# The q scores of an agent-attention kernel, each 126-token tile computed as four 32-column tiles of the array

## The chip, the cores and the metric

The kernel runs on one core of a Trainium2 chip. The metric is the device time of one execution in microseconds (us). The time before is 2154.62 us, the median of three runs (2154.03 to 2154.73). A profile of one execution, with a span of 2150.6 us from the first to the last instruction, is what the readings below come from.

The engines are named as the profile names them: PE is TensorE's matmul, PEld its weight load, DVE is VectorE, ACT is ScalarE, POOL is GpSimd and SP is SyncE, which issues DMAs.

## The reference

Attention through 49 agents, then a two-layer network on 49920 tokens of width 128:

```python
B, N, C = (4, 12480, 128)
n_agents = 49
def sm(a, b):
    s = scale * (a @ b.transpose(0, 2, 1))
    s = s - s.max(-1, keepdims=True)
    e = np.exp(s)
    return e / (e.sum(-1, keepdims=True) + 1e-09)
a2k = sm(agents, k)
agent_v = a2k @ v
q2a = sm(q, agents)
out = (q2a @ agent_v)
...
h = x @ w_in          # 128 x 2048
g = h - np.tanh(h)
return (g @ w_out)    # 2048 x 128
```

The change concerns `q @ agents.T`, the scores of each token against its batch's 49 agents ("q scores").

## The kernel before

The tokens of each of the four batches are cut into 25 blocks of 500 (the last has 480), 100 blocks in all. The main loop runs over blocks and, within a block, over eight pairs of 128-wide slices of the 2048 hidden columns. In a step `m1` computes the hidden slice pair `h` in PSUM from the block's q softmax `pT` (lines 534 and 535: a high and a low part of the combined weights, so that two fast matmuls stand for one exact one). `act` computes `z` on ScalarE and `g` on VectorE (lines 544 to 549), `high` rounds `g` to `gh` on GpSimd (line 578), `low` takes the difference `gl` on VectorE (line 583), and `m2` adds the three products of `gh` and `gl` with the high and low parts of `w_out` to the block's sum (lines 596 to 598). Every other block computes one pair in plain fp32 instead (line 594), without `gh` and `gl`.

Beside this stream run jobs, Python generators that are advanced by one `yield` a step. For each pair of blocks a q job (`q_softmax`) makes the softmax of eight tiles of 126 tokens: the scores on TensorE (line 490), their maximum "qm" on VectorE (line 498), a copy on ScalarE, the subtraction on GpSimd, the exponential, the sums "qs" and the division on VectorE (lines 505 to 508), and the split into "pp" (lines 511 and 513). Later jobs transpose "pp" to `pT` (line 521). While a batch's blocks run, further jobs compute the next batch's agent side: its key scores (line 278), transposes (line 329) and value sums (line 339). Lines 249 and 369 are the first batch's, before the main loop starts.

In line 490 the stationary operand is a 126-token piece of `qt` (128 x 126) and the moving one is `ag` (128 x 49). Both are fp32, and each such matmul leaves two records in the profile. In line 278 the keys' scores are written to two halves of the PSUM partitions, each from a 64-column stationary operand:

```python
to = ps[HALF * r : HALF * (r + 1), c * 128 : (c + 1) * 128]
nc.tensor.matmul(to, self.agz[:, b, :], kt[:, n // 2 * r + c, :], start=True, stop=True)
```

The PSUM tile `misc` has two buffers, shared by the block sums, the q scores, the transposes and the agent side. `h` has three. The order on each engine in the main part is made by a scheduler from the order of the code and from its own estimates of durations, so a changed instruction can move others.

Of the kernel before, what the change touches and what calls it, by code (L numbers as in the profile page):

```python
# [24 lines left out]
A = 49  # L25
A2 = 2 * A
EARLY = 11
HALF = 64
FF = 2048
NCH = FF // 128  # L30
TT = 126
# [6 lines left out]
BT = GT // 2  # L38
# [58 lines left out]
class Build:  # L97
# [19 lines left out]
    def constants(self):  # L117
        nc = self.nc
        c = self.const
        self.agz = c.tile([128, B, HALF], F32, tag="ag", name="ag")  # L120
        self.ag = self.agz[:, :, :A]
# [6 lines left out]
        self.sel = c.tile([128, A], F32, tag="sel", name="sel")  # L128
        for r in (slice(0, HALF), slice(HALF, 128)):
            nc.vector.tensor_copy(self.sel[r], self.ident[r, r.start : r.start + A])  # L130
# [3 lines left out]
        nc.vector.memset(self.mx, 0.0)  # L134
        self.w_in = c.tile([128, FF], F32, tag="w_in", name="w_in")
        self.wo_h = c.tile([128, NCH, C], F32R, tag="wo_h", name="wo_h")
# [58 lines left out]
    def phase1(self, b):  # L195
# [36 lines left out]
        def scores(g):  # L232
# [42 lines left out]
            for c in range(n // 2):  # L275
                for r in range(2):
                    to = ps[HALF * r : HALF * (r + 1), c * 128 : (c + 1) * 128]
                    nc.tensor.matmul(to, self.agz[:, b, :], kt[:, n // 2 * r + c, :], start=True, stop=True)  # L278
# [4 lines left out]
        def max_in():  # L283
            yield
            yield
            if b:
                m = self.small.tile([128, 1], F32, tag="mk", name="mk")
                top = self.small.tile([128, 1], F32, tag="mt", name="mt")
                nc.vector.tensor_reduce(m, st["mxp"], axis=AX.X, op=ALU.max)
                nc.vector.tensor_copy(top[:HALF], m[HALF:])  # L290
                nc.vector.tensor_tensor(m[:HALF], m[:HALF], top[:HALF], ALU.max)
                nc.vector.tensor_copy(m[HALF:], m[:HALF])
                st["mb"] = self.small.tile([128, 1], F32, tag="mn", name="mn")
# [148 lines left out]
    def project(self, b, bound):  # L442
        nc = self.nc

        def part(c, lo, hi):
            yield
            yield
            if c == 0:
                self.aw[b] = tuple(
                    self.keep.tile([128, FF], F32R, tag=t, name=t, bufs=2) for t in ("awh", "awl")  # L450
                )
# [32 lines left out]
    def q_softmax(self, halves, qt, res, TT=TT):  # L484
        nc = self.nc
        ps = self.misc()
        for t in range(GT):
            b, at, w = halves[t // BT]
            at += min(t % BT * TT, w - TT)
            nc.tensor.matmul(ps[:TT, t * A : (t + 1) * A], qt[:, at : at + TT], self.ag[:, b, :], start=True, stop=True)  # L490
            if t % BT == BT - 1:
                yield
        pv = ps[:TT, : GT * A].rearrange("p (t a) -> p t a", a=A)
        m = self.small.tile([128, GT], F32, tag="qm", name="qm")
        e = self.small.tile([128, GT, A], F32, tag="qe", name="qe")
        ev = e[:TT]
        s = self.small.tile([128, GT], F32, tag="qs", name="qs")
        nc.vector.tensor_reduce(m[:TT], pv, axis=AX.X, op=ALU.max)
        nc.scalar.copy(ev, pv)  # L499
        yield  # L500
        nc.gpsimd.tensor_tensor(ev, ev, m[:TT, :, None].broadcast_to([TT, GT, A]), ALU.subtract)  # L501
        yield
        nc.scalar.activation(ev, ev, AF.Exp, scale=SCALE)
        yield
        nc.vector.tensor_reduce(s[:TT], ev, axis=AX.X, op=ALU.add)
        nc.vector.tensor_scalar(s[:TT], s[:TT], EPS, None, ALU.add)
        nc.vector.reciprocal(s[:TT], s[:TT])
        nc.vector.tensor_tensor(ev, ev, s[:TT, :, None].broadcast_to([TT, GT, A]), ALU.mult)
        yield
        pp = self.small.tile([128, GT, A2], F32R, tag="pp", name="pp")  # L510
        nc.scalar.copy(pp[:TT, :, :A], ev)  # L511
        yield
        nc.gpsimd.tensor_tensor(pp[:TT, :, A:], ev, pp[:TT, :, :A].bitcast(F32), ALU.subtract)  # L513
        res.append(pp)
# [119 lines left out]
    def fast(self):  # L634
# [21 lines left out]
        with ExitStack() as first:  # L656
# [6 lines left out]

            self.wf = self.keep.tile([128, FF], F32R, tag="awh", name="awh", bufs=2).bitcast(F32)
            loads = []
# [237 lines left out]
```

## Time and profile before

| what | value |
|---|---|
| median of three runs | 2154.62 us |
| span of the profiled execution | 2150.6 us |
| TensorE busy | 2126.8 us, 99% of the span |
| VectorE busy | 1998.3 us, 93% |
| ScalarE busy | 1828.1 us, 85% |
| GpSimd busy | 1313.8 us, 61% |
| matmul records | 10859 |
| line 490: matmuls | 800 records, 93.4 us busy, mean 269 ns |
| line 490: weight loads | 800 records, 95.9 us busy, mean 190 ns |
| line 490's share of the chain that ended last | 4% |
| mean granted TensorE clock | 0.998 |

The runs' own time lies some 4 us above the span of the profiled execution, which starts at the first instruction and ends with the last. In the profile's rows "x16" is the count of records merged into one row, "128\*126 128x49 f32" is the array's active rows and columns and the moving operand. Matmul bars overlap: a bar lasts longer than the distance to the next start, and its end is modelled. A stretch of matmuls is therefore measured from start to start.

### The profile page before, as it was taken

The page shows a single profiled execution, that of the slowest core. Times are in us where ns is not written, and L with a number is a line of the kernel's source. Part 1 is how long each engine was busy: PE and PEld are TensorE (multiplying, and loading weights), DVE is VectorE, ACT ScalarE, POOL GpSimd, SP SyncE. Part 2 cuts the span into 40 slices and gives each one's busy share as a digit, 9 for nine tenths or more (in the row PEclk, how much of TensorE's full clock was granted, in tenths as well). Part 3 has the DMA queues.
Part 4 walks back from the last instruction along what each step waited for, and adds up shares of the span by engine and source line. Part 5 has one row for each costly group of instructions (what it writes and reads, how often), then busy time and mean ns, then how long its engine had stood idle before and what let it go on. Part 6 is the DMA issues. An engine that isn't in the chain of part 4 may idle for free.

```text
span 2150.6 us, 30293 instructions
## 1 busy us (share of the span) xinstructions
PE 2126.8 (99%) x10859; PEld 1713.6 (80%) x10859; DVE 1998.3 (93%) x2031; ACT 1828.1 (85%) x2136; POOL 1313.8 (61%) x858
## 2 busy tenths in 40 slices
PE   8999999999999999999999999999999999999998
PEld 7587878877877887888787778878878888888886
DVE  7999998889999998889999999988999999999998
ACT  3888888888888888888898888888889889899896
POOL 0365566556665565556675557655566767777666
PEclk9999999999999999999999999999999999999999
DMA  9321112110111111111002110111000000000000
GB/s 350 96 67 60 52 34 73 51 49 29 39 49 59 60 50 49 59 61 49 20 20 68 59 42 28 51 59 41 28 31 20 29 30 20 29 29 20 29 10 21
DMA packets 65325, 108.69 MB, mean 51 GB/s; under 512 B 3984, under 2 KB 44176, under 8 KB 65168
## 3 DMA queue, kind: packets, MB, share of 16 engines
q1 hardware_dynamic: 65168, 106.68, 15.1%
q8 instruction: 89, 1.46, 0.3%
q14 instruction: 68, 0.56, 0.1%
HBM read 81.10 MB, written 25.56 MB: 50 GB/s over the span
## 4 chain that ended last, share of the span: by engine, by line
PE 95%; DVE 2%; POOL 1%; issue 1%; ACT 0%; DMA 0%; POOLq 0%; SPq 0%; DVEq 0%
PE h L534 17%; PE h L535 16%; PE misc L598 16%; PE misc L596 15%; PE misc L597 15%; PE misc L594 4%; PE misc L490 4%; PE misc L339 2%; PE misc L278 2%; PE misc L521 1%; PE h L249 1%; POOL gh L578 1%; DVE g L549 1%; PE misc L329 1%; DVE gl L583 1%
## 5 line engine op out<-in xcount | busy, mean ns | idle before, releaser
L578 POOL TENSOR_SCALAR gh<-g 128x1000 fp32r<-128x1000 f32 (+1 forms) x743 | 1172.7, 1579 | 702.9 <-DVE g L549 357.9
L583 DVE TENSOR_TENSOR gl<-g,gh 128x1000 fp32r<-128x1000 f32 (+1 forms) x743 | 952.8, 1284 | 99.9 <-PE misc L598 58.9
L549 DVE TENSOR_TENSOR g<-h,z 128x1000 f32<-128x1000 f32 (+1 forms) x800 | 946.1, 1187 | 24.6 <-ACT z L546 20.6
L544 ACT ACTIVATE y<-h 128x1000 f32<-128x1000 f32 (+1 forms) x800 | 799.0, 1002 | 191.6 <-PE h L535 187.6
L546 ACT ACTIVATE z<-y 128x1000 f32<-128x1000 f32 (+1 forms) x800 | 828.8, 1040 | 21.2 <-DVE g L549 4.2
L534 PE MATMUL h<-pT,awh 98*128 98x500 f32 (+1 forms) x1600 | 662.1, 414 | 0.1
L535 PE MATMUL h<-pT,awl 98*128 98x500 f32 (+1 forms) x1600 | 623.1, 389 | 0.0
L598 PE MATMUL misc<-gl,wo_h 128*128 128x500 f32 (+1 forms) x1486 | 589.5, 397 | 3.7 <-DVE gl L583 3.7
L596 PE MATMUL misc<-gh,wo_l 128*128 128x500 f32 (+1 forms) x1486 | 579.0, 390 | 2.8 <-POOL gh L578 2.8
L597 PE MATMUL misc<-gh,wo_h 128*128 128x500 f32 (+1 forms) x1486 | 578.1, 389 | 0.0
L534 PEld LDWEIGHTS h<-pT,awh 98*128 98x128 f32 x1600 | 301.2, 188 | 77.4 <-issue 14.0
L535 PEld LDWEIGHTS h<-pT,awl 98*128 98x128 f32 x1600 | 303.0, 189 | 67.7 <-issue 14.7
L598 PEld LDWEIGHTS misc<-gl,wo_h 128*128 128x128 f32 x1486 | 279.1, 188 | 70.0 <-DVE gl L583 10.5
L596 PEld LDWEIGHTS misc<-gh,wo_l 128*128 128x128 f32 x1486 | 280.8, 189 | 62.6 <-POOL gh L578 7.8
L597 PEld LDWEIGHTS misc<-gh,wo_h 128*128 128x128 f32 x1486 | 279.7, 188 | 54.5
L501 POOL TENSOR_TENSOR qe<-qe,qm 126x392 f32<-126x392 f32 x50 | 69.7, 1395 | 65.3 <-ACT qe L499 65.3
L513 POOL TENSOR_TENSOR pp<-qe,pp 126x392 fp32r<-126x392 f32 x50 | 67.8, 1357 | 58.4 <-ACT pp L511 56.6
L490 PEld LDWEIGHTS misc<-ag,qt 128*126 128x126 f32 x800 | 95.9, 190 | 3.9
L490 PE MATMUL misc<-ag,qt 128*126 128x49 f32 x800 | 93.4, 269 | 0.0
L594 PE MATMUL misc<-g,wo_f 128*128 128x500 f32 (+1 forms) x196 | 89.9, 581 | 0.0
L754 ACT ACTIVATE o<-misc 128x500 f32<-128x500 f32 (+1 forms) x100 | 58.2, 582 | 21.7 <-PE misc L598 11.7
L526 ACT CAST pT<-misc 98x500 fp32r<-98x500 f32 (+1 forms) x100 | 56.7, 568 | 7.4 <-PE misc L521 6.5
(111 smaller groups left out, 840.5 us busy)
## 6 DMA issues: line engine op xcount, KB each, us to landing
kt<-kT SPq DMA_DIRECT2D x48, 512.0 KB, 3.7
qt<-qT SPq DMA_DIRECT2D x46, 500.0 KB, 3.4
outT<-o SPq DMA_DIRECT2D x46, 500.0 KB, 2.6
v<-v SPq DMA_DIRECT2D x36, 512.0 KB, 4.1
vt<-v SPq DMA_DIRECT2D x12, 512.0 KB, 7.1
raw<-w_in SPq DMA_DIRECT2D x4, 512.0 KB, 9.0
v<-w_out SPq DMA_DIRECT2D x4, 512.0 KB, 8.9
qt<-qT SPq DMA_DIRECT2D x4, 490.0 KB, 3.4
```

What stands on the lines that cost most here:

```text
L490: nc.tensor.matmul(ps[:TT, t * A : (t + 1) * A], qt[:, at : at + TT], self.ag[:, b, :], start=True, stop=True)
L534: nc.tensor.matmul(h[:, c, :w], aw[0][:A2, sl], pT[:A2, :w], start=True, stop=False)
L535: nc.tensor.matmul(h[:, c, :w], aw[1][:A2, sl], pT[:A2, :w], start=False, stop=True)
L544: nc.scalar.activation(self.pair(y), h, AF.Tanh, scale=TSC)
L546: nc.scalar.activation(z, y, AF.Square)
L549: nc.vector.tensor_tensor(self.pair(g), h, self.pair(z), ALU.mult)
L578: self.nc.gpsimd.tensor_scalar(gh, g, 1.0, 0.0, ALU.mult, ALU.add)
L583: self.nc.vector.tensor_tensor(gl, g, gh.bitcast(F32), ALU.subtract)
L594: nc.tensor.matmul(acc[:, :w], wf[:, c * C : (c + 1) * C], gh[:, x], start=first, stop=last)
L596: nc.tensor.matmul(acc[:, :w], self.wo_l[:, f, :], gh[:, x], start=first, stop=False)
L597: nc.tensor.matmul(acc[:, :w], self.wo_h[:, f, :], gh[:, x], start=False, stop=False)
L598: nc.tensor.matmul(acc[:, :w], self.wo_h[:, f, :], gl[:, x], start=False, stop=last)
```

## The change

Each matmul of line 490 becomes four, of 32, 32, 32 and 30 tokens, which write to partitions 0, 32, 64 and 96 onward of the same PSUM columns. The output partitions select a group of 32 columns of the array, so the four are column tiles with a stationary operand of 32 (30) columns each. The moving operand is the same 128 x 49 for all. The `yield` that stood between the first four and the last four token tiles goes behind all eight, so the number of yields stays two.

```diff
+QUART = 32
...
         for t in range(GT):
             b, at, w = halves[t // BT]
             at += min(t % BT * TT, w - TT)
-            nc.tensor.matmul(ps[:TT, t * A : (t + 1) * A], qt[:, at : at + TT], self.ag[:, b, :], start=True, stop=True)
-            if t % BT == BT - 1:
-                yield
+            for r in range(0, TT, QUART):
+                m = min(QUART, TT - r)
+                to = ps[r : r + m, t * A : (t + 1) * A]
+                nc.tensor.matmul(to, qt[:, at + r : at + r + m], self.ag[:, b, :], start=True, stop=True)
+        yield
+        yield
```

The lines behind it move down by four: line 490 is line 494 in the changed kernel, 498 is 502, 534 is 538, 583 is 587, 596 to 598 are 600 to 602.

On TensorE, in the middle of the main loop, a job's scores stood as one row of eight matmuls between two steps' work:

```order
L598 MATMUL misc<-gl,wo_h 128x500
L596 MATMUL misc<-gh,wo_l 128x500
L597 MATMUL misc<-gh,wo_h 128x500
L490 MATMUL misc<-ag,qt 126x49 x8
L534 MATMUL h<-pT,awh 128x500
L535 MATMUL h<-pT,awl 128x500
```

In the changed kernel the same place holds eight times the first two of these score rows (32 matmuls), and the next work behind them is often the block sum's instead of a new `h`:

```order
L601 MATMUL misc<-gh,wo_h 128x500
L494 MATMUL misc<-ag,qt 32x49 x3
L494 MATMUL misc<-ag,qt 30x49
...
L602 MATMUL misc<-gl,wo_h 128x500
L600 MATMUL misc<-gh,wo_l 128x500
```

So the eight stay together, as they did, with four times as many instructions. In two of the 50 jobs they don't. There four matmuls of the block sum stand between the first and the last part of the changed kernel's scores on TensorE:

```order
L602 MATMUL misc<-gl,wo_h 128x500
L600 MATMUL misc<-gh,wo_l 128x500
L601 MATMUL misc<-gh,wo_h 128x500
L602 MATMUL misc<-gl,wo_h 128x500
L494 MATMUL misc<-ag,qt 32x49 x3
L494 MATMUL misc<-ag,qt 30x49
L600 MATMUL misc<-gh,wo_l 128x500
```

The job whose tail this is has 28 of its 32 matmuls ahead of these four; the other such job has 14 ahead and 18 behind.

On VectorE, the steps of a q job in the last third of the main loop stood like this before (`g` and `gl` are the stream's, "qm", "qs" and "qe" the job's):

```order
L549 TENSOR_TENSOR g<-h,z 128x1000
L498 TENSOR_REDUCE qm<-misc 126x8
L549 TENSOR_TENSOR g<-h,z 128x1000
L583 TENSOR_TENSOR gl<-g,gh 128x1000 x2
L505 TENSOR_REDUCE qs<-qe 126x8
L549 TENSOR_TENSOR g<-h,z 128x1000
L506 TENSOR_SCALAR qs<-qs 126x8
```

and stand like this in the changed kernel:

```order
L553 TENSOR_TENSOR g<-h,z 128x1000
L502 TENSOR_REDUCE qm<-misc 126x8
L587 TENSOR_TENSOR gl<-g,gh 128x1000 x2
L553 TENSOR_TENSOR g<-h,z 128x1000 x2
L509 TENSOR_REDUCE qs<-qe 126x8
L587 TENSOR_TENSOR gl<-g,gh 128x1000
L510 TENSOR_SCALAR qs<-qs 126x8
```

The reduction "qm" keeps its place behind a `g`; one `g` of the stream moves from ahead of the two `gl` to behind them, and the sum "qs" comes one place later. The order of the DMAs on SP is the same.

## The prediction

> **What bounds the kernel now.** I read the page first: the span, the busy shares and the shares of the chain that ended last.
>
> ```profile
> span 2150.6 us, 30293 instructions
> PE 2126.8 (99%) x10859; PEld 1713.6 (80%) x10859; DVE 1998.3 (93%) x2031; ACT 1828.1 (85%) x2136; POOL 1313.8 (61%) x858
> PE 95%; DVE 2%; POOL 1%; issue 1%; ACT 0%; DMA 0%; POOLq 0%; SPq 0%; DVEq 0%
> ```
>
> TensorE is busy all the time and is the chain for 95% of it. "Busy" can mislead here, because a matmul's bar is longer than the distance to the next one. So I measured by starts, and I looked at stages for the engine that would come second.
>
> ```profile
> 85.00:300.00 215.00, 212.18 (x1104) 167.76 (x1105) 205.69 (x204) 182.44 (x213) 133.19 (x90) 1.00 0.17 55
> 300.00:1550.00 1250.00, 1248.21 (x6488) 1004.86 (x6487) 1151.84 (x1153) 1074.10 (x1255) 759.21 (x499) 1.00 0.15 47
> 1550.00:2076.00 526.00, 525.58 (x2437) 428.85 (x2436) 509.18 (x492) 469.07 (x525) 369.00 (x228) 1.00 0.08 26
> ```
>
> The columns are the stretch, then busy PE, PEld, DVE, ACT and POOL, then the granted clock. TensorE binds in all three. VectorE stands close behind: 205.69 of 215 (95.7%), 1151.84 of 1250 (92.1%) and 509.18 of 526 (96.8%). The clock is 1.00 throughout, so no term below needs a correction for it. Before 85 us TensorE also waits for loads and for VectorE; the first two of the 50 q jobs lie there, and I count what they save as nothing.
>
> The same view of line 490 alone counts the jobs behind that:
>
> ```profile
> 85.00:300.00 215.00, 9.27 (x80) 9.57 (x80) 1.00 0.17 55
> 300.00:1550.00 1250.00, 53.79 (x464) 55.51 (x464) 1.00 0.15 47
> 1550.00:2076.00 526.00, 24.12 (x208) 25.06 (x209) 1.00 0.08 26
> ```
>
> One fp32 matmul leaves two records, so a job of 8 matmuls leaves 16. That is 5, 29 and 13 jobs, and one more that straddles 2076: 48. The timeline of TensorE round one of them:
>
> ```profile
> 244.51 0.40 PE L597 MATMUL misc<-gh,wo_h 128*128 128x500 f32 x1
> 244.74 1.85 PE L490 MATMUL misc<-ag,qt 128*126 128x49 f32 x16
> 246.42 0.47 PE L534 MATMUL h<-pT,awh 98*128 98x500 f32 x1
> 246.73 0.39 PE L535 MATMUL h<-pT,awl 98*128 98x500 f32 x1
> ```
>
> All 16 records run together although the code yields after four tiles: the scheduler has merged the halves already. Neighbouring 500-column matmuls start 0.23 us apart, so without the group L534 would have led L535 by 0.23 us. The group costs from 244.51 + 0.23 = 244.74 to 246.73 - 0.23 = 246.50: **1.76 us**, or 0.110 us a record. The chain has such groups in full ("1.69", and 0.07 more on the matmul behind):
>
> ```profile
> 1801.04 1.69 PE misc L490 x16
> 1802.73 0.30 PE h L534
> ```
>
> **What a record of the group is limited by.** The price of a streamed column comes from four fp32 matmuls of 500 columns:
>
> ```profile
> 256.13 1.84 PE L594 MATMUL misc<-g,wo_f 128*128 128x500 f32 x4
> 257.41 0.79 PE L535 MATMUL h<-pT,awl 98*128 98x500 f32 x1
> 258.03 0.39 PE L534 MATMUL h<-pT,awh 98*128 98x500 f32 x1
> ```
>
> From 256.13 to 258.03 - 0.23 = 257.80 is 1.67 us, 0.418 a record, 0.84 ns a column. The 49 columns of q scores therefore stream in 41 ns, and the record takes 110. The rest must be the weights: 126 of them, 0.87 ns each. That is what four column tiles can attack: 32 weights would load in 28 ns, below the 41 ns of the stream.
>
> **The change, step by step.** It replaces 16 records by 64 (8 token tiles x 4 column tiles x 2), each with its own weight load. No row shows 32-column tiles. The nearest are the 64-column ones of line 278, which put two tiles side by side:
>
> ```profile
> 253.08 0.39 PE L597 MATMUL misc<-gh,wo_h 128*128 128x500 f32 x1
> 253.40 1.09 PE L278 MATMUL misc<-kt,ag 128*64 128x128 f32 x16
> 254.42 0.50 PE L534 MATMUL h<-pT,awh 98*128 98x500 f32 x1
> 254.76 0.39 PE L535 MATMUL h<-pT,awl 98*128 98x500 f32 x1
> 261.00 0.38 PE L598 MATMUL misc<-gl,wo_h 128*128 128x500 f32 x1
> 261.31 0.44 PE L278 MATMUL misc<-kt,ag 128*64 128x128 f32 x4
> 261.68 0.50 PE L596 MATMUL misc<-gh,wo_l 128*128 128x500 f32 x1
> 262.02 0.39 PE L597 MATMUL misc<-gh,wo_h 128*128 128x500 f32 x1
> ```
>
> By the same reckoning the group of 16 costs 254.53 - 253.31 = 1.22 us and the group of 4 costs 261.79 - 261.23 = 0.56. Twelve records are 0.66 us, 0.055 each; what is left, 0.56 - 4 x 0.055 = **0.34 us, is a fixed price of a tiled group** (it starts late, and the matmul behind has its weights exposed). An untiled group has none: the q group's 1.76 is 16 x 0.110. Each 278 record streams 128 columns, 107 ns, and two of them take 2 x 55 = 110: the two tiles run at once, at full rate each, with 2 to 3 ns lost. The first moments of the group, in a window of 30 ns, say so too:
>
> ```profile
> 253.40 0.14 PEld L278 LDWEIGHTS misc<-kt,ag 128*64 128x64 f32 x2 [0.35 <-ACT y L544]
> 253.40 0.33 PE L278 MATMUL misc<-kt,ag 128*64 128x128 f32 x2
> ```
>
> Two loads together last 0.14 us, and one alone has a mean of 136 ns on this line: the loads run side by side as well.
>
> If four tiles do what two do, each tile works through its own 16 records at max(41, 28) + 3 = 44 ns: 0.70 us, plus 0.34 fixed = **1.04 us instead of 1.76, 0.72 saved**. The bounds of this unknown: below, 41 ns and a fixed price shorter by half a 64-weight load (28 ns): 0.97; above, four tiles that take turns, in the rivals.
>
> The Trainium skill speaks against it. "TensorEngine Tiling (Array Packing)", Performance Considerations, says that a matmul has an overhead of about 60 cycles on TRN2 whatever its free dimension, and not to tile a dimension that is small already; "TensorE: Matmul & The Clock Gate", Part 1, gives about 25 ns as the least distance between two starts. By that floor 64 starts would take 1.60 us and the group 1.94, an estimate from that page. The two rows above, with two starts inside 30 ns, don't agree with it across tiles, but no run here shows a long train of such starts.
>
> The sum: 5 + 29 + 14 jobs at 0.72. In the first two stages VectorE has the room (215 - 3.6 = 211.4 against 205.7; 1250 - 20.9 = 1229.1 against 1151.8): 3.6 + 20.9 = 24.5 us. In the last, 526 - 14 x 0.72 = 515.9 leaves VectorE 98.7% busy (509.18), so I count two thirds of 10.1: 6.7. In the changed order two jobs are cut in two by four matmuls of another line; each cut pays the fixed price once more, -0.7. The steps of a job are otherwise moved by a place or so, VectorE's reduction "qm" among them. It now waits for the group:
>
> ```profile
> 1842.85 0.57 DVE L498 TENSOR_REDUCE qm<-misc 126x8 f32<-126x392 f32 x1 [0.65 <-PE misc L490]
> ```
>
> A shorter group makes that wait shorter; I add nothing for it, since VectorE isn't the bound. The DMAs, SP's and POOL's queues keep their work and their order up to a step. In all 24.5 + 6.7 - 0.7 = 30.5: the span goes to 2120.1. The median lies 2154.62 - 2150.6 = 4.0 us above the span, so the time is **2124.1 us**. Alone, this case runs from 2115 (0.79 us saved in all 50 jobs) to 2136 (nothing passed on in the first and last stage, 20.9 - 0.7 saved, and a little for waits in the new order).
>
> **The rivals.** *Two tiles at a time.* The trace shows never more than two at once. Four in two turns make 88 ns a row of four: 16 x 0.088 + 0.34 = 1.75 us, nothing gained: 2155, within 5 either way. For it: nothing but the absence of a row. Against: two lose only 2 to 3 ns to each other.
>
> *One shared path, slower.* If the four weight loads take turns, a row costs 4 x 28 = 112 ns: 1.79 + 0.34 = 2.13, 0.37 more in 48 jobs, +18 and 0.7 for the cuts: 2173. If the four streams take turns, 4 x 44 = 176: 3.16 us, +68: 2223. It decides from 88 ns a row upward. Against it stand the two loads and the two matmuls of 253.40.
>
> *Issue is the bound.* Four times as many instructions come in one burst. The densest train in the trace is line 369's:
>
> ```profile
> 38.00:43.00 5.00, 5.00 (x96) 5.00 (x94) 1.00 0.86 279
> ```
>
> About 92 pairs of load and matmul start in these 5 us, 54 ns a pair, and there the streams set the pace. Were 54 the limit, 64 pairs would take 3.46 + 0.34 = 3.80, +2.04 a job, +98: 2253. The turning point is (1.76 - 0.34) / 64 = 22 ns a pair. By the floor of 25 ns on the skill's page the estimate is +0.18 a job, about 2164.
>
> *VectorE takes over, or the scheduler undoes it.* The first is priced in the sum (at worst 2136); the second is the two cut jobs, 0.7 us.
>
> **How the numbers follow.** Four at once, VectorE's share of the loss included: 0.70. Two at a time or near it: 0.11. Loads or streams in turn: 0.09. Issue: 0.10. What a measurement of this kernel can tell from no change is about 0.2%, 4.3 us. Faster: 0.70 and a third of the second case, for rows between 44 and 80 ns: 0.74. Same: 0.08. Slower: 0.18. The range takes in the first case and the second up to 95 ns a row (16 x 0.095 + 0.34 = 1.86, +5): 2114 to 2159.
>
> **What would show it.** Right: 64 records of the q line in a group that costs about 1.04 us by starts (0.34 fixed, and rows 44 ns apart between), 3200 records in all, and a chain still led by TensorE; VectorE's busy time unchanged near 1998 us and its share up to 94 to 95%. Wrong: rows at 88 ns or more; a group that runs its first records fast and the rest at a slower pace (issue); or a group of 1.04 us with TensorE idle elsewhere, waiting for "gl" or for "h" to be freed, which would put the loss on VectorE or on the new order.

## The result and the profile after

The changed kernel takes 2141.97 us (median of four runs, 2141.54 to 2142.99) against 2154.68 before: a ratio of 0.9941, 95% interval 0.9927 to 0.9955. It is 12.7 us faster, where 30.5 had been forecast.

First the page of the changed kernel: the span, the busy shares, and the shares of the chain that ended last.

```profile
span 2141.2 us, 35133 instructions
PE 2107.2 (98%) x13259; PEld 1658.2 (77%) x13259; DVE 1996.0 (93%) x2031; ACT 1820.5 (85%) x2136; POOL 1303.9 (61%) x858
PE 66%; DVE 18%; issue 6%; POOL 5%; ACT 4%; DMA 0%; POOLq 0%; SPq 0%; DVEq 0%; ACTq 0%
```

TensorE led the chain for 95% before and leads it for 66% now. VectorE has gone from 2% to 18%, though its busy time is what it was (1998.3 us before, 1996.0 now). So other engines now end waits that TensorE's own work ended before.

The timeline of TensorE around one group of scores, early in the main loop:

```profile
243.99 0.39 PE L539 MATMUL h<-pT,awl 98*128 98x500 f32 x1
244.31 0.90 PE L494 MATMUL misc<-ag,qt 128*32 128x49 f32 x64
245.13 0.49 PE L602 MATMUL misc<-gl,wo_h 128*128 128x500 f32 x1
245.47 0.39 PE L600 MATMUL misc<-gh,wo_l 128*128 128x500 f32 x1
```

By the prediction's reckoning the group costs 245.47 - 0.23 - (243.99 + 0.23) = 1.02 us. The median of the main loop's 46 whole groups of 64 records is 1.03 us (1.76 for the 48 groups of 16 before): 1.04 had been forecast. The first 35 ns of this group, by themselves:

```profile
244.31 0.25 PE L494 MATMUL misc<-ag,qt 128*32 128x49 f32 x4
```

Four column tiles start in that stretch. By the single starts, the four of a row come 5 to 7 ns apart, and the next row follows 43 ns after the row before (medians over these groups). Their four weight loads start 5 to 7 ns apart too and last 0.11 us each, so they run side by side. The tiles do what they were meant to do. The loss lies elsewhere, and the list of waits shows where TensorE's weight loads stand, before and after:

```profile
PEld misc L598 <- DVE gl L583: 10.5, 21, 1.3
PEld misc L596 <- POOL gh L578: 7.8, 14, 1.1
```

```profile
PEld misc L602 <- DVE gl L587: 23.1, 46, 1.2
PEld misc L600 <- POOL gh L582: 21.6, 35, 1.2
```

The columns are the total in us, the count, and the longest. The two waits have grown by 26.4 us together. To place the loss I took the times at which ScalarE copies a block's finished sum out, and compared stretches of blocks (a q job belongs to two blocks). Blocks 72 to 97, from 1620 to 2110 us before, are most of the prediction's last stage. "Column tiles, order of before" is the first experiment below.

| stretch, us | before | after | column tiles, order of before |
|---|---|---|---|
| start to first block's end | 83.0 | 85.3 | 84.1 |
| blocks 0 to 8 | 175.0 | 173.0 | 172.2 |
| blocks 8 to 24 | 340.1 | 336.7 | 334.4 |
| blocks 24 to 72 | 1022.4 | 1015.5 | 1004.1 |
| blocks 72 to 97 | 489.1 | 490.1 | 483.7 |
| behind them | 40.9 | 40.6 | 40.7 |
| span of the profiled execution | 2150.6 | 2141.2 | 2119.2 |

The gain is small in each stretch from block 0 to 72, and in blocks 72 to 97 nothing is left of it. By the spans the gain is 9.4 us, by the medians 12.7. That is so because each run's time lies 1.8 us above its own span: the execution that was profiled before (span 2150.6) took about 2152.4, some 2 us less than the median, and the changed kernel's profiled one 2142.99, 1.0 more. Before, the spans of further runs beside the experiments lie from 2149.7 to 2154.5. So I read nothing into 1 or 2 us in the first row.

### The profile page after: what moved, and what is told of

Same layout as the page of the kernel before. It is cut to its first block, busy times and chain, and to the rows that moved or that the text cites. A ratio compares the mean times of both kernels' runs of the same rounds, so it can differ in the third digit from the quotient of the medians.

```text
span 2141.2 us, 35133 instructions
## 1 busy us (share of the span) xinstructions
PE 2107.2 (98%) x13259; PEld 1658.2 (77%) x13259; DVE 1996.0 (93%) x2031; ACT 1820.5 (85%) x2136; POOL 1303.9 (61%) x858
## 4 chain that ended last, share of the span: by engine, by line
PE 66%; DVE 18%; issue 6%; POOL 5%; ACT 4%; DMA 0%; POOLq 0%; SPq 0%; DVEq 0%; ACTq 0%
PE misc L602 12%; PE h L538 11%; PE misc L600 11%; PE h L539 11%; PE misc L601 10%; DVE g L553 9%; DVE gl L587 6%; POOL gh L582 4%; PE misc L598 3%; ACT y L548 2%; PE misc L340 2%; PE misc L494 2%; ACT z L550 1%; PE misc L279 1%; PE h L250 1%
## 5 line engine op out<-in xcount | busy, mean ns | idle before, releaser
L582 POOL TENSOR_SCALAR gh<-g 128x1000 fp32r<-128x1000 f32 (+1 forms) x743 | 1197.8, 1612 | 690.2 <-DVE g L553 387.5
L587 DVE TENSOR_TENSOR gl<-g,gh 128x1000 fp32r<-128x1000 f32 (+1 forms) x743 | 956.5, 1287 | 85.6 <-PE misc L602 42.9
L602 PEld LDWEIGHTS misc<-gl,wo_h 128*128 128x128 f32 x1486 | 279.0, 188 | 83.3 <-DVE gl L587 23.1
L600 PEld LDWEIGHTS misc<-gh,wo_l 128*128 128x128 f32 x1486 | 280.6, 189 | 75.3 <-POOL gh L582 21.6
L505 POOL TENSOR_TENSOR qe<-qe,qm 126x392 f32<-126x392 f32 x50 | 46.9, 938 | 77.2 <-ACT qe L503 77.2
L517 POOL TENSOR_TENSOR pp<-qe,pp 126x392 fp32r<-126x392 f32 x50 | 55.6, 1113 | 59.6 <-ACT pp L515 59.5
L598 PEld LDWEIGHTS misc<-g,wo_f 128*128 128x128 f32 x196 | 36.9, 188 | 26.2 <-issue 22.5
L525 PEld LDWEIGHTS misc<-identr,pp 126*98 126x98 f32 x400 | 38.9, 127 | 18.4 <-POOL pp L517 6.5
```

The lines of the kernel that those rows point to most:

```text
L582: self.nc.gpsimd.tensor_scalar(gh, g, 1.0, 0.0, ALU.mult, ALU.add)
L587: self.nc.vector.tensor_tensor(gl, g, gh.bitcast(F32), ALU.subtract)
L598: nc.tensor.matmul(acc[:, :w], wf[:, c * C : (c + 1) * C], gh[:, x], start=first, stop=last)
L600: nc.tensor.matmul(acc[:, :w], self.wo_l[:, f, :], gh[:, x], start=first, stop=False)
L602: nc.tensor.matmul(acc[:, :w], self.wo_h[:, f, :], gl[:, x], start=False, stop=last)
```

## The experiments

Two theories stood against each other. The **VectorE theory** (theory 1 in the expectations): TensorE's groups are shorter, so VectorE, second in every stage, ends the waits. The **order theory** (theory 2): the scheduler gave the engines another order, because a job's scores are 32 instructions to it where they were eight, and that order costs what is missing. The order printed from the built program, which needs no run, shows that the yields aren't what moved things: with the old yields and 32 matmuls the scheduler makes the changed kernel's order, and with the new yields and eight it makes the old one (but for the very first job's scores). Before, 37 of the main loop's 48 groups had matmuls of the next hidden pair right behind them, all four in 25 of these. In the changed kernel all 46 whole groups have a block sum's six first, and behind the six come two hidden pairs in 44. ScalarE's runs of two tanh and then two squares ("y y z z", of two steps) went from 54 to 97, and VectorE's "gl gl g g" from 75 to 102.

To set an order apart from the matmuls, each experiment below chains the instructions of the main part on TensorE, VectorE, ScalarE and GpSimd to a written list, with a tile's four score matmuls as one unit:

```diff
+    def follow(self, first):
...
+            mine.sort(key=lambda x: x[:2])
+            for (_, _, a), (_, _, b) in zip(mine, mine[1:]):
+                self.tc.add_manual_dep(b, a.name, info, reason="a given order")
```

### Column tiles in the order of before

The edit: line 494's four matmuls stay, and all engines follow the order that the kernel before had.

> The four column tiles of the changed kernel, but with every instruction on TensorE, VectorE, ScalarE and GpSimd in the order of the kernel before. Theory 1 (VectorE and what it shares with GpSimd and ScalarE is the next bound, whatever the order): the scores group stays at 1.03 us, and the time stays within 4 us of the changed kernel's 2142. Theory 2 (the scheduler, which sees 32 matmuls where it saw 8, wrote a worse order, and that took the gain): 2118 to 2128, most of the 35 us that 48 groups save on TensorE.

Measured: 2121.11 us (2120.94 to 2122.19), ratio 0.9845 (0.9828 to 0.9861). The same matmuls at the same work are 20.9 us faster in the old order. Its groups cost 1.03 us. The page's chain and the two waits:

```profile
PE 88%; DVE 7%; issue 2%; POOL 2%; ACT 1%; DMA 0%; POOLq 0%; SPq 0%; DVEq 0%
...
PEld misc L612 <- POOL gh L594: 11.6, 20, 1.0
PEld misc L614 <- DVE gl L599: 9.9, 22, 1.3
```

Against the changed kernel, TensorE's waits for gh are down from 21.6 to 11.6 us and those for gl from 23.1 to 9.9. The order theory holds.

### Whole matmuls in the new order

```diff
-            for r in range(0, TT, QUART):
...
-                nc.tensor.matmul(to, qt[:, at + r : at + r + m], self.ag[:, b, :], start=True, stop=True)
+            nc.tensor.matmul(ps[:TT, t * A : (t + 1) * A], qt[:, at : at + TT], self.ag[:, b, :], start=True, stop=True)
```

All engines follow the changed kernel's order.

> The undivided matmuls of the kernel before, with every instruction in the order of the changed kernel. Groups of 1.76 us again. Theory 1: 2150 to 2158, as the kernel before. Theory 2: slower than the kernel before by the order's own price, 2165 to 2178.

Measured: 2174.86 us, ratio 1.0089 (1.0072 to 1.0106). The four cells fit together: the tiles bring 33.6 us in the old order (2154.7 to 2121.1) and 32.9 in the new (2174.9 to 2142.0). The order costs 20.2 with whole matmuls and 20.9 with tiles. The two effects add. The chaining itself has no visible price: the chained run is the faster one in the first difference and the slower one in the second, so a price of the chain would have set 33.6 and 32.9 apart.

### VectorE made lighter, in the new order and in the old

```diff
-        nc.vector.tensor_reduce(m[:TT], pv, axis=AX.X, op=ALU.max)
+        nc.vector.tensor_reduce(m[:TT], pv[:, :, :7], axis=AX.X, op=ALU.max)
```

The sum and the division are cut to seven agents in the same way, so these kernels leave out 42 of the 49 agents in the softmax. The first run keeps the changed kernel's order, the second is on the old one.

> The changed kernel in its own order, held fixed, with the maximum, the sum and the division of the q softmax on VectorE taken over 7 of the 49 agents only (the other 42 enter neither the maximum nor the sum and are not divided), which leaves out some 1.2 us of VectorE's work in each of 50 jobs. Theory 1: the time falls by most of what TensorE has spare, to 2118 to 2128. Theory 2 (waits come from the order, not from VectorE's load): it falls by less than 10 us, 2132 to 2142.

> Four column tiles in the order of the kernel before, with VectorE's maximum, sum and division of the q softmax over 7 of the 49 agents only (the others enter neither the maximum nor the sum and are not divided), some 1.2 us of VectorE less in each job. If TensorE is the bound again with the old order: little to gain, 2112 to 2120, mostly in the last stage, where blocks passed 38.70 us a job against 38.40 that TensorE needs. If VectorE is the bound throughout: below 2105.

Measured: 2132.82 us in the new order (0.9895, 0.9879 to 0.9912) and 2113.33 in the old (0.9811, 0.9794 to 0.9829): 9.2 and 7.8 less than with the full VectorE. The places differ. In the new order 7.0 of it come in blocks 8 to 72 (1352.2 to 1345.2) and 0.7 in the last stage; in the old 1.8 and 3.6. So VectorE's time does count in the new order, in stages where the prediction gave it room. In the new order's last stage (1550 to 2076 us) the lighter VectorE mostly waits longer for ScalarE's `z`, 16.0 us where it had waited 8.2, which points at ScalarE there. But even with the lighter VectorE the orders stand 19.5 us apart, so VectorE's load alone doesn't explain the loss.

### One engine's order at a time

TensorE follows the new order, the other three the old.

> Four column tiles; TensorE in the order of the changed kernel, VectorE, ScalarE and GpSimd in the order of the kernel before. If TensorE's order alone makes the price (behind the scores it does the block sums first and the new hidden slices, which ScalarE waits for, only then): 2136 to 2146, as the changed kernel's 2142. If the other engines' orders make it: 2119 to 2126, as with all of the old order (2121.1).

Measured: 2214.32 us, ratio 1.0281 (1.0263 to 1.0299), far from both expectations. TensorE then asks for results in an order in which the other engines don't make them; its weight loads' wait for `gl` is 68.7 us, so this tells nothing of TensorE's part in the 20.9 us. Other mixes were not run.

### Two column tiles in the old order

Against the changed kernel:

```diff
-            for r in range(0, TT, QUART):
-                m = min(QUART, TT - r)
+            for r in range(0, TT, HALF):
+                m = min(HALF, TT - r)
```

> Two column tiles of 64 and 62 tokens instead of four, every engine in the order of the kernel before. If the weight load sets a row (64 x 0.87 = 56 ns, 58 with the loss between records): a group of 16 x 0.058 + 0.34 = 1.27 us, 0.49 saved in 48 jobs, and with the share that came through with quarters (33.6 of 35) 2130 to 2134. If the stream of 49 columns or the issue of instructions sets it, 44 ns or less: a group of about 1.04 and 2119 to 2124.

Measured: 2134.47 us, ratio 0.9908 (0.9891 to 0.9926), just above the 2130 to 2134 expected. The group costs 1.26 us, its rows 58 ns apart (median), as expected. With 64 (62) weights a tile, the load sets the row (64 x 0.87 = 56 ns), as the prediction had it for 126; with 32 the stream sets it (41 ns, 43 measured).

### The hidden pair behind the group, first and late

In the first run the new order gets the next hidden pair right behind the scores again; in the second the old order has it moved behind the block sum in 25 jobs. On TensorE, the second reads:

```diff
-L550 MATMUL h<-pT,awh 128x500
-L551 MATMUL h<-pT,awl 128x500
...
 L612 MATMUL misc<-gh,wo_l 128x500
 L613 MATMUL misc<-gh,wo_h 128x500
+L550 MATMUL h<-pT,awh 128x500
+L551 MATMUL h<-pT,awl 128x500
```

> The changed kernel in its own order on every engine but for one place: in the 44 jobs in which TensorE does six block sums and then eight matmuls of two hidden pairs behind the scores, the first hidden pair's four matmuls now come right behind the scores, ahead of the six. If ScalarE's wait for a late hidden pair makes the order's price (20.9 us): 2120 to 2131. If the price lies in the order of VectorE, ScalarE and GpSimd: no change, 2138 to 2146.

> The reverse: four column tiles in the order of the kernel before, but in the 25 jobs in which TensorE does one hidden pair and then six block sums behind the scores, the six sums come first. If the late hidden pair is the price: slower than 2121 by about half of 20.9 us, 2128 to 2136. If not: 2119 to 2125.

Measured: 2141.21 us (0.9939, 0.9922 to 0.9955), no change, and 2129.03 (0.9879, 0.9863 to 0.9896), 7.9 slower than the old order. Moving the pair late costs 7.9 us in the old order; moving it first brings nothing back in the new one. By the second run alone the pair would have passed for the price; the first says that it isn't. So the place of this pair isn't the price by itself.

### ScalarE's pairs

93 times in the new order, "y y z z" becomes "y z y z", where z is the square that VectorE's `g` needs:

```diff
 L560 ACTIVATE y<-h 128x1000
-L560 ACTIVATE y<-h 128x1000
 L562 ACTIVATE z<-y 128x1000
+L560 ACTIVATE y<-h 128x1000
 L562 ACTIVATE z<-y 128x1000
```

Why this was tried shows in a timeline of the changed kernel's last stage (ScalarE and VectorE):

```profile
1842.84 1.01 ACT L548 ACTIVATE y<-h 128x1000 f32<-128x1000 f32 x1 [0.35 <-PE h L539]
...
1843.75 1.96 ACT L550 ACTIVATE z<-y 128x1000 f32<-128x1000 f32 x2
1844.81 1.20 DVE L553 TENSOR_TENSOR g<-h,z 128x1000 f32<-128x1000 f32 x1 [0.69 <-ACT z L550]
```

The first of the two squares comes one tanh (1.01 us) later than it could, and VectorE, the engine with the least room, stands for 0.69 us. The second run also puts the hidden pair first.

> The changed kernel in its own order, but wherever ScalarE did two first steps (y, y) and then two second steps (z, z) of the hidden stream, 93 places, it now does them alternately (y, z, y, z). VectorE's product g waits for z, and in the new order for some 0.7 us in each job of the last stage. If that is the order's price: 2121 to 2132. If it is a lag that the other engines' places keep up: 2136 to 2146.

> Both edits at once: ScalarE alternates, and TensorE does the first hidden pair right behind the scores. If the two places together make the price, which neither made alone: 2121 to 2130. If it lies on VectorE and GpSimd: 2136 to 2146.

Measured: 2129.97 us (0.9889, 0.9872 to 0.9905), 12.0 faster than the changed kernel, and 2129.63 (0.9884, 0.9868 to 0.9901), which is the same. VectorE's `g` in the window from 1550 to 2076 us, grouped by line, in the changed kernel and then in the alternating one (busy us and mean ns, then idle time ahead and what ended it):

```profile
L553 DVE TENSOR_TENSOR g<-h,z 128x1000 f32<-128x1000 f32 (+1 forms) x214 | 253.0, 1187 | 8.2 <-ACT z L550 8.2
```

```profile
L565 DVE TENSOR_TENSOR g<-h,z 128x1000 f32<-128x1000 f32 (+1 forms) x218 | 256.9, 1183 | 0.0
```

VectorE's 8.2 us of waiting for z are gone. Blocks 72 to 97 take 481.2 us instead of 490.1: 8.9 of the 12.0, and 2.5 less than the old order's 483.7. A window of that stage shows TensorE now almost without a gap (399.69 of 400 us), in the changed kernel and then the alternating one (the columns as in the prediction):

```profile
1650.00:2050.00 400.00, 397.36 (x2338) 314.58 (x2337) 387.13 (x368) 354.61 (x400) 279.06 (x175) 1.00 0.07 25
```

```profile
1650.00:2050.00 400.00, 399.69 (x2369) 322.38 (x2368) 394.28 (x376) 360.42 (x407) 284.75 (x178) 1.00 0.07 25
```

What is left of the order's price lies in blocks 8 to 72: 1349.7 against 1338.5 us.

### The same alternation in the old order

> The column tiles in the order of before, and in it the 52 places where ScalarE copies y y z z turned to y z y z. If the alternation is what lets TensorE run at its own floor in the last stage, this gains there what the old order with its pairs still loses: some 38.4 us a job there instead of 38.7, in all 2113 to 2119. If the alternation only repairs something that the new order broke, it stands at the 2121.1 of the old order or a little behind: 2119 to 2124.

Measured: 2120.52 us (2120.39 to 2120.97), ratio 0.9847 (0.9831 to 0.9864): no change against 2121.11. The 52 pairs in the old order cost nothing, and VectorE's wait for z in its last stage stays at 3.5 us. So ScalarE's pairs aren't bad in themselves. Where they cost, as far as the runs show, is the new order's last stage, in which VectorE's next instruction is the `g` that needs the delayed square.

### VectorE's pairs taken apart

On top of ScalarE's alternation, 100 places of "gl gl g g" become "gl g gl g".

> The changed kernel's order with ScalarE alternating (2130.0 alone), and VectorE's 100 places of gl gl g g turned to gl g gl g. If VectorE's pairs are what makes gh and gl late for the second matmuls in the middle stages (some 11 us of waits over blocks 24 to 72 that the old order doesn't have), those waits go: 2119 to 2126. If they are not, nothing moves: 2128 to 2132.

Measured: 2136.25 us (0.9919, 0.9903 to 0.9936), 6.3 slower than without. A miss, and the waits say how:

```profile
DVE g L565 <- ACT z L562: 118.4, 126, 2.5
...
PEld misc L614 <- DVE gl L599: 36.5, 70, 1.7
...
PEld misc L612 <- POOL gh L594: 8.4, 12, 1.2
```

The waits for gh fell (14.4 us with ScalarE's alternation alone, 8.4 now), but those for gl grew from 19.3 to 36.5, and VectorE waits 118.4 us for z where it waited 19.2: a `g` that is moved ahead of a `gl` asks for a square that isn't there yet, and the ready `gl` stands behind it.

### What is left: VectorE's room in the new order

The alternating new order, with the lighter VectorE.

> The changed kernel's order with ScalarE alternating (2130.0), and VectorE's maximum, sum and division of each q job over 7 of the 49 agents, so that its output is not the softmax. What is left of the new order's price against the old one is 8.9 us, as waits for gh and gl in blocks 8 to 72. If these waits are VectorE's lack of room in the new order, the lighter VectorE takes most of them away, some 7 us there (as it did in the changed kernel), and about 1 in the last stage: 2120 to 2124. If ScalarE's pairs and VectorE's load were the same loss counted twice, little is left to gain: 2127 to 2131. The old order with the light VectorE stands at 2113.3, so a time of 2113 to 2117 would say that the order has no price but through these two.

Measured: 2120.02 us (0.9845, 0.9829 to 0.9862). This is 10.0 less than with the full VectorE, at the edge of what VectorE's room should give, and not at 2113 to 2117. Blocks 8 to 72 take 1341.8 us; the old order with the lighter VectorE takes 1336.7. So the new order's price there is 11.2 us with the full VectorE (1349.7 to 1338.5) and 5.1 with the lighter one: 6.1 go with VectorE's load. Another 2.2 of the 10.0 are the start's (83.9 to 81.7 us), as in the old order (84.1 to 81.8).

How VectorE's load turns into a wait of TensorE shows in a timeline of the changed kernel, in the stage before the last:

```profile
607.18 1.20 DVE L553 TENSOR_TENSOR g<-h,z 128x1000 f32<-128x1000 f32 x1
608.29 1.20 DVE L587 TENSOR_TENSOR gl<-g,gh 128x1000 fp32r<-128x1000 f32 x1
608.56 1.82 POOL L582 TENSOR_SCALAR gh<-g 128x1000 fp32r<-128x1000 f32 x1 [0.40 <-DVE g L553]
609.40 1.20 DVE L553 TENSOR_TENSOR g<-h,z 128x1000 f32<-128x1000 f32 x1
610.51 0.69 DVE L282 TENSOR_REDUCE mxk<-misc 128x1 f32<-128x512 f32 x1
610.78 1.04 POOL L582 TENSOR_SCALAR gh<-g 128x1000 fp32r<-128x1000 f32 x1 [0.40 <-DVE g L553]
611.11 1.76 DVE L587 TENSOR_TENSOR gl<-g,gh 128x1000 fp32r<-128x1000 f32 x1
612.79 1.19 DVE L553 TENSOR_TENSOR g<-h,z 128x1000 f32<-128x1000 f32 x1
613.89 1.18 DVE L587 TENSOR_TENSOR gl<-g,gh 128x1000 fp32r<-128x1000 f32 x1
614.15 1.83 POOL L582 TENSOR_SCALAR gh<-g 128x1000 fp32r<-128x1000 f32 x1 [2.33 <-PE misc L601]
...
616.04 0.19 PEld L600 LDWEIGHTS misc<-gh,wo_l 128*128 128x128 f32 x1 [0.74 <-POOL gh L582]
```

The reduction "mxk" of the agent side takes 0.69 us on VectorE. It also lets `gh` start before `gl`, and the `gl` behind it lasts 1.76 instead of 1.19. The steady beat is 2.22 us from one `g` to the next (607.18 to 609.40); the next comes 3.39 later, 1.17 late. GpSimd has stood for 2.33 us when it starts the next `gh`, 0.17 us behind that `g`, as far behind it as the two `gh` before it (the row names a matmul that ended at the same time). TensorE's weight load then waits 0.74 us for this `gh`. The next two `g` follow after 2.21 and 2.22 us more, so nothing of the 1.17 us is made up there. This is one place; how many of the waits arise in this way was not counted.

## Why the prediction went wrong, point by point

**The group: right.** Forecast 1.04 us, measured 1.03; rows 43 ns apart, where 44 had been worked out; 3200 records. "Two at a time", "one shared path" and "issue" are out: four tiles start within some 20 ns, their loads and streams run side by side, and 64 matmuls start in 0.69 us, first to last (11 ns a start, where the issue rival turned at 22). The Trainium skill, in "TensorEngine Tiling (Array Packing)", Performance Considerations, advises against taking a tiling factor from a dimension that is already small. The prediction took that to speak against the change, but what is cut here is the 126 columns of the stationary operand; the small dimension, the 49 moving columns, stays whole. The floor that the Trainium skill gives in "TensorE: Matmul & The Clock Gate", Part 1, about 25 ns between starts, doesn't hold across column tiles in this trace, where starts lie 5 to 7 ns apart.

**The sum of the gain: right where the order was kept.** 24.5 + 6.7 = 31.2 was forecast without the cuts. In the old order 33.6 were measured; by the table 26.8 of it lie in blocks 0 to 72 and 5.4 in 72 to 97. The first stretch has 36 jobs, at 0.73 us each 26.3, so there all of it came through. The second has 12, 8.8 us: 5.4 of them passed, a share of 0.61 where two thirds had been chosen, and the lighter VectorE brings 3.6 more there, about what is missing. So VectorE did take its part of the last stage's gain. The fixed price of 0.34 us a group held too (1.03 - 16 x 0.043). The 4.0 us between span and median were a mistake of 2: a run lies 1.8 above its own span, and the profiled one was a quicker one. It doesn't touch the gain.

**The step that failed: "the steps of a job are otherwise moved by a place or so", with two cuts at 0.7 us for all that the scheduler does.** The section on the change showed the two `gl` of VectorE's rows moving ahead of a `g` and the block sum moving ahead of `h`, and the prediction priced both at nothing but "a little for waits in the new order". The order costs 20.9 us with the tiles and 20.2 without them, six tenths of what the tiles earn. The rival "VectorE takes over, or the scheduler undoes it" gave the second half 0.7 us, and so missed where the risk lay. The case listed last under what would show it, "a group of 1.04 us with TensorE idle elsewhere", is what happened; it had no price of its own.

**Where the 20.9 us go.** ScalarE's pairs in the new order: 12.0 by the run that takes them apart, 8.9 of it in the last stage, where VectorE had no room to wait for a late square, and 2.5 in blocks 8 to 72. The rest is in blocks 8 to 72, as waits for gh and gl: some 6 us go away with a lighter VectorE, and some 5 stay. Which moved instruction these 5 hang on is open. Moving the late hidden pair first brought nothing on top of ScalarE's alternation, and taking VectorE's pairs apart as was tried cost 6.3 us, which doesn't say what another order of them would do. The causes overlap, so the shares hold in the order in which they were taken away. The alternation also made the last stage 2.5 us faster than the old order's, which offsets part of this rest.

**VectorE's room: too coarse.** The prediction gave VectorE room in the first two stages by its busy share (95.7% and 92.1%) and priced only the last. A share below 100% says that VectorE can keep up on the whole, not that each `gl` and `gh` is in time. With the lighter VectorE the changed kernel gained 7.0 us in blocks 8 to 72, which lie mostly in stages where the sum counted VectorE as free. In the old order it gained 1.8 there: with that order VectorE's room was nearly enough.

**The best version** is the column tiles in the order of before, 2121.1 us, with or without ScalarE's alternation (2120.5). The forecast of 2124.1 would have been near for this version. The range of the prediction, 2114 to 2159, holds the result, but that is luck: its upper part was drawn for slower rows of tiles, and the rows were as fast as forecast.

## What to carry to other kernels

Where a scheduler sets the order, a change in the number of instructions is two changes: take them apart in a two by two, old and new instructions, each in the old and the new order. Where the engines behind the bound are over 90% busy, a busy share is no slack: look at what the engine with the least room does next, and price every place where the new order makes its input later. Taking 93 pairs apart on ScalarE, which is 85% busy, was worth 12 us here.

## What the runs showed of the hardware that was not expected

**GpSimd's `gh` and VectorE's `gl` shut each other out.** In the rows from 608.29 on, `gh` takes 1.82 us where it starts behind a `gl`, and 1.04 where it starts beside a reduction; the `gl` that starts behind this `gh` takes 1.76. In the whole trace of the changed kernel, the median of `gh` is 1.82 us in the 584 cases with over 0.5 us of a `gl` beside it, and 1.04 in 156 cases with none, among them 148 with a `g` beside it. The median of `gl` is 1.19 where it starts first (519), 1.20 with no `gh` beside it (156) and 1.87 where `gh` starts first (68). So whichever comes second is held up by the first, while `g`, which reads one operand from PSUM, leaves `gh` at 1.04 us. The Trainium skill, "SBUF — State Buffer", section "SBUF: two separate sides", tells of such a lock: a pair of ports that a GpSimd operation or a VectorE operation with two SBUF inputs holds for a whole instruction, whichever starts first, while the other is blocked. The trace agrees: `gh` grows by 0.78 us, `gl` by 0.68. The prediction left it out. It can turn a small move into a delay, as in the timeline, where it makes 0.57 of the 1.17 us. But in sum `gl` is busy 956.5 us in the changed kernel and 957.4 in the old order with the tiles, so the lock by itself doesn't make the order's price.

**TensorE's clock is halved in stretches of the start, and in more of them after the change.** Windows of TensorE alone, before and after (the clock is the first figure behind the brackets):

```profile
35.00:40.00 5.00, 5.00 (x74) 0.76 0.48 136
...
55.00:60.00 5.00, 4.53 (x16) 1.00 1.04 375
```

```profile
35.00:40.00 5.00, 5.00 (x64) 0.57 0.39 111
...
55.00:60.00 5.00, 5.00 (x10) 0.52 1.02 394
```

At 55 to 60 us TensorE of the changed kernel does fewer matmuls (10 records against 16) in more busy time, at half the clock. Its stretches at half clock sum to 13.7 us in the profiled execution, against 3.4 before. (The last microseconds of each execution, also at half clock, are left out.) In the old order with tiles one such stretch of 3.4 us lies around 54 us, and with ScalarE's alternation in that order they sum to 10.2 us. What sets them off wasn't tried by itself, and whether they belong to an order or to the single execution stays open. They come in lengths of 3.4 us and twice that, which agrees with the window of about 3.4 us that the Trainium skill gives in "TensorE: Matmul & The Clock Gate", Part 1.
